# Other places in memory for the attention weights of a fused attention and feed-forward kernel, with the buffers rearranged that make room

## Chip, core and metric

The kernel runs on one core of a Trainium2 chip. The metric is the device time of one execution in microseconds (us); the kernel before took 703.69 us (median of three runs, 703.57 to 704.2).

## What is computed

A slot attention over 8 batches, 8 heads, 576 tokens, 64 dimensions and 32 slots is followed by a feed-forward layer of width 2048 with an ELU.

```
a = exp(phi - max over tokens);  a = a / (sum over tokens + 1e-9)
k_m, v_m = a^T k, a^T v                        # 32 slots per head
attn = softmax over slots of (q k_m^T / 8)
x = attn v_m                                   # all heads side by side, 4608 x 512
h = x w_in;  g = where(h > 0, h, exp(min(h, 0)) - 1)
out = g w_out                                  # 4608 x 512
```

## The kernel before

The values v_m of a batch are multiplied with `w_in` first (`vw`), so the hidden layer is the attention weights times `vw`. A batch has two halves of 288 tokens; a unit of work is one batch, one half and one of 16 tiles of 128 hidden channels: 256 units. From unit 8 on, every factor is split into a high and a low part in the fast float32 format, and a product is made of three passes: low weights with high stream, high with low, high with high (`PASSES`).

`hidden` (L1005) is the first matmul group of a unit: three passes for two groups of heads, six matmuls. The weights are `vw`; the stream is a part of the attention-weight tile `A`, whose shape is [128, group, high or low, 288] in 4-byte numbers. `elu_exp` (L1020, L1021, on ScalarE) makes the exponential into a buffer `gf` out of the accumulator `psh`; `elu_max` (L1029 or L1032, VectorE) finishes it in place; `elu_high` (L1044) and `elu_low` (L1050) split its first 256 tokens into `gp`. The last 32 tokens of a half are collected in `rest`, for the first batches by `rest_copy` on GpSimd (L1040), and are projected later with others (`rest_high`, `rest_project`). `project` (L1058) streams 512 columns of `wout` for two token tiles and three passes: six matmuls, with `gp` as weights. The units before number 8 use plain float32 for both (`hidden` L993, `project` L1077).

The order of all this is written out by hand: `ORDER` is a list of steps, each of which records its instructions, and every engine runs its own in that order. A pool gives a new tile the room of one whose readers have all been recorded, and the first writer of the new tile waits for them.

Small things around: `phi_max` and `phi_exp` leave a negated maximum and a sum per slot in `stats`; `slot_scale` makes the reciprocal `rinv`. From batch 2 on, the maxima go through DRAM and come back spread over all partitions in `nmx` (`send_max`, `spread_max`); `pick_max` copies the half that a partition needs to `nmb`, on GpSimd, and `e_shift` (L531, GpSimd) adds it to three thirds of a second copy of phi, loaded by `load_e` into tiles of the rotating tag `t2k`. `softmax_max` and `softmax_sum` keep maxima and sums of the attention weights in a tile `mx`.

In the built program the four A tiles begin on multiples of 256 bytes, before and after.

Of the kernel before, what the change touches and what calls it, by code (L numbers as in the profile page):

```python
# [8 lines left out]
F32 = mybir.dt.float32  # L9
F32R = mybir.dt.float32r  # L10
U32 = mybir.dt.uint32
AF = mybir.ActivationFunctionType
# [4 lines left out]
P = 128  # L17
B, H, S, D, M = 8, 8, 576, 64, 32
DM, DFF = 512, 2048
HALF = S // 2  # L20
# [4 lines left out]
UT = S // NU  # L25
SQ = 32
NSQ = 2 * UT // SQ
NB = 2
# [384 lines left out]
def fused_kernel(ctx: ExitStack, tc: tile.TileContext, phiT, phi, kv0, kvt, kv1, kv2, q0, q1, w_in, w_out, out):  # L413
# [8 lines left out]
    nc = tc.nc  # L422

    const = ctx.enter_context(tc.tile_pool(name="const", bufs=1))
    work = ctx.enter_context(tc.tile_pool(name="work", bufs=2))
# [5 lines left out]
    ident = const.tile([P, P], F32, name="ident")  # L431
# [4 lines left out]
    def t2k(shape, name):  # L436
        return work.tile(shape, F32, name=name, tag="t2k", bufs=7)

    tiny = work.tile([P, HALF], F32, name="gf", bufs=5)[:, 0:1]
    spare = [work.tile([P, 4 * CW], F32, name="spare", tag="vw", bufs=NVB) for _ in range(2)]
    SPARE = {"e0": 0, "e1": 512, "e2": 1024, "x0": 1536, "x1": 1664, "sc0": 2048, "sc1": 2368,
             "sc2": 2624, "sc3": 2944, "A320": 3200, "A321": 2048}
# [4 lines left out]
    def temp(b, name, i, n):  # L449
# [20 lines left out]
    st = [  # L470
        {"kv": {}, "q": {}, "vw": [None] * NVC, "A": [None, None], "e": {}, "sc": {}, "ps": {}}
        for _ in range(B)
    ]
# [24 lines left out]
        st[b]["ph"] = t  # L498

    def load_e(b, u):  # L500
        t = t2k([P, 3, P], "e")
        nc.sync.dma_start(t, phi[b - NB, :, 3 * u : 3 * u + 3])
        st[b]["e"][u] = t

    def send_max(b):

# [3 lines left out]
    def spread_max(b):  # L510

        s = st[b]
        d = s.pop("nmd")
        s["nmx"] = work.tile([P, P, 2], F32, name="nmx", bufs=1)
        nc.sync.dma_start(
            s["nmx"].rearrange("p x a -> p (x a)"),
            d.rearrange("x a -> (x a)").partition_broadcast(P),
        )

    def pick_max(b):  # L520

        s = st[b]
        s["nmb"] = work.tile([P, P], F32, name="nmb", bufs=1)
        for a in range(2):
            r = slice(a * TT, a * TT + TT)
            nc.gpsimd.tensor_copy(s["nmb"][r], s["nmx"][r, :, a])
# [139 lines left out]
    def phi_max(b, g=None):  # L666
        s = st[b]
        if "nm" not in s:
            s["nm"], s["sums"], s["rinv"] = (stats[:, b % 2, i] for i in range(3))
        g = slice(0, 2) if g is None else slice(g, g + 1)  # L670
        nc.vector.tensor_reduce(s["nm"][:, g], s["ph"][:, g], AX.X, ALU.max, negate=True)

# [7 lines left out]
    def slot_scale(b):  # L680
        s = st[b]
        sums = s["sums"]
        nc.vector.tensor_scalar(sums, sums, EPS, None, ALU.add)
        nc.vector.reciprocal(s["rinv"], sums)

    def e_transpose(b, u, where="b"):
# [132 lines left out]
    def turn(b, u, a):  # L819
# [5 lines left out]
        sc = s["sc"][u].rearrange("p n m -> p (n m)")  # L825
        nc.vector.transpose(sc[:, a * n : (a + 1) * n], s["ps"]["s", u][a])

    def softmax_max(b, u):
        sc = st[b]["sc"][u]
        n = sc.shape[1]  # L830
        t = work.tile([P, 2, 2 * UT // SQ], F32, name="mx")[:, :, :n]
        mx = t[:, 0]
        st[b]["sm", u] = t
        nc.vector.tensor_reduce(mx, sc, AX.X, ALU.max)  # L834
        st[b]["mx", u] = mx

# [11 lines left out]
    def softmax_sum(b, u):  # L848
        sc = st[b]["sc"][u]
        n = sc.shape[1]  # L850
        t = st[b].pop(("sm", u))
        sm = t[:, 1]
        nc.vector.tensor_reduce(sm, sc, AX.X, ALU.add)  # L853
        nc.vector.tensor_scalar(sm, sm, EPS, None, ALU.add)
        rs = sm
        nc.vector.reciprocal(rs, sm)
        st[b]["rs", u] = rs
# [32 lines left out]
            t0 = t1  # L890

    def new_A():
        return work.tile([P, 2, 2, HALF], F32R, name="A", bufs=4)

    def half_high(b, hf):
        s = st[b]
        s["A"][hf] = new_A()
        nc.scalar.copy(s["A"][hf][:, :, HI], s["A32"][hf])
# [5 lines left out]
    def probs_high(b, u):  # L904
        s = st[b]
        for hf, src, dst in probs_parts(b, u):
            if s["A"][hf] is None:
                s["A"][hf] = new_A()
            nc.scalar.copy(s["A"][hf][:, :, HI, dst], s["pr", u][:, :, src])
# [106 lines left out]

    def elu_exp(it):
        ps = gs[it]
        gf = work.tile([P, HALF], F32, name="gf", bufs=5)
        nc.scalar.activation(gf, ps, AF.Relu, scale=-1.0)  # L1020
        nc.scalar.activation(gf, gf, AF.Exp, scale=-1.0)  # L1021
        gs[it] = gf, ps
# [152 lines left out]
        eng = nc.scalar if p == B // 2 - 1 else nc.sync  # L1175
        eng.dma_start(rows, osbs.pop(("rest", p)))

    stats = work.tile([P, 2, 3, 2], F32, name="stats", bufs=1)
    work.tile([P, 2, 2 * UT // SQ], F32, name="mx")
    warm = ps_o.tile([P, P], F32, name="pso00")  # L1180

    def tables():
        nc.scalar.activation(tiny, ident[:, 0:1], AF.Exp)

    def warm_up(n):
        for _ in range(n):
# [5 lines left out]
    def pad(n):  # L1192
# [4 lines left out]
        f.__name__: f  # L1197
        for f in (
            tables, warm_up, pad, load_phi, load_e, load_kv, load_kv0, load_tail, load_q, load_half_q, load_raw, dec_mag,
            dec_low, dec_top, dec_add, dec_high, dec_rest, phi_max, phi_exp, slot_scale,  # L1200
            send_max, spread_max, pick_max, e_shift, e_exp, e_transpose, e_copy, slots, slots_copy, slots_transpose,
            kv_copy, all_scores, pair_scores, scores, turn, softmax_max, softmax_shift, softmax_exp, softmax_sum,
            softmax_divide, turn_back, probs_high, probs_low, vw, vw_copy, half_high, half_low, vw_high, vw_low, hidden,
            elu_exp, elu_max, rest_copy, elu_high, elu_low, project, project_part, collect_part, store_part, collect, store, rest_high, rest_low,
            rest_project, rest_collect, rest_store,
        )
# [53 lines left out]
```

## Time and profile before

| | |
|---|---|
| median of three runs | 703.69 us (703.57 to 704.2) |
| profiled execution | 703.95 us |
| its span, first to last instruction | 702.2 us |
| TensorE busy | 694.2 us, 99% |
| VectorE, ScalarE, GpSimd busy | 478.2, 461.4, 51.2 us |
| granted clock of TensorE | 1.000 of full speed |

Busy time of TensorE counts overlapping records once; a record lasts longer than the step to the next one. DMA moves 64.51 MB.

### The profile page before, as it was taken

To read this page: it belongs to the slowest core of one execution; us is meant where nothing else is said; L and a number is where in the kernel's file an instruction comes from. 1 tells how busy PE (TensorE), PEld (TensorE's weight loads), DVE (VectorE), ACT (ScalarE), POOL (GpSimd) and SP (SyncE) were. 2 spreads that over 40 slices of the span, in tenths; PEclk is the share of its full clock that TensorE was granted. 3 is DMA by queue.
4 is the path that set the end of the run, shared out by engine and by line. 5 is a ranking of instruction groups with operands and counts; after the bars stand their busy time and mean duration, and the time that the engine had idled before them with its cause. 6 is when DMAs were issued, how large, how long until landed. Compare 5 with 4: busy or idle time off the path is not lost.

```text
span 702.2 us, 14394 instructions
## 1 busy us (share of the span) xinstructions
PE 694.2 (99%) x5521; PEld 572.5 (82%) x5521; DVE 478.2 (68%) x1253; ACT 461.4 (66%) x1104; POOL 51.2 (7%) x100
## 2 busy tenths in 40 slices
PE   9999999999999999999999999999999999999997
PEld 8656787888788887888878888888878888888886
DVE  3999999896886488645954459644875457755443
ACT  3788898887665667756674557665675656756553
POOL 0011112113120002000100000200010000000000
PEclk9999999999999999999999999999999999999999
DMA  8992014434940534004211043103211010000001
GB/s 296 375 414 80 29 31 120 155 106 98 238 162 15 177 102 107 30 16 140 76 47 46 9 141 120 38 1 137 79 54 46 1 47 1 32 31 1 1 30 46
DMA packets 24261, 64.51 MB, mean 92 GB/s; under 512 B 3264, under 2 KB 6592, under 8 KB 24192
## 3 DMA queue, kind: packets, MB, share of 16 engines
q1 hardware_dynamic: 24048, 63.32, 27.6%
q8 instruction: 44, 0.72, 0.4%
q10 hardware_dynamic: 144, 0.26, 0.1%
q14 instruction: 25, 0.20, 0.1%
HBM read 54.13 MB, written 9.44 MB: 91 GB/s over the span
## 4 chain that ended last, share of the span: by engine, by line
PE 90%; DVE 7%; ACT 2%; issue 1%; POOL 0%; DVEq 0%; POOLq 0%
PE pso L1058 48%; PE psh L1005 27%; PE psb L1058 5%; PE psb L785 3%; PE psb L717 2%; PE pso L785 2%; PE pso L1187 1%; DVE top L626 1%; DVE gf L1029 1%; DVE win L650 1%; DVE top L625 0%; DVE mx L853 0%; ACT gf L1021 0%; DVE mx L834 0%; PE psb L770 0%
## 5 line engine op out<-in xcount | busy, mean ns | idle before, releaser
L1058 PE MATMUL pso<-wout,gp 128*128 128x512 f32 (+1 forms) x1515 | 389.2, 393 | 0.0
L1058 PEld LDWEIGHTS pso<-wout,gp 128*128 128x128 f32 x1515 | 270.1, 188 | 48.6 <-ACT gf L1021 1.7
L1005 PEld LDWEIGHTS psh<-A,vw 128*128 128x128 f32 x1488 | 220.3, 188 | 34.7 <-issue 6.1
L1005 PE MATMUL psh<-A,vw 128*128 128x288 f32 x1488 | 238.6, 296 | 0.6 <-DVE gf L1029 0.4
L1044 ACT CAST gp<-gf 128x256 fp32r<-128x256 f32 x248 | 100.2, 404 | 93.8 <-DVE gf L1032 77.0
L1032 DVE SCALAR_TENSOR_TENSOR gf<-gf,psh 128x256 f32<-128x256 f32 x192 | 80.3, 418 | 107.4 <-ACT gf L1021 106.4
L1020 ACT ACTIVATE gf<-psh 128x288 f32<-128x288 f32 x256 | 105.1, 410 | 70.6 <-PE psh L1005 67.4
L1050 DVE TENSOR_TENSOR gp<-gf,gp 128x256 fp32r<-128x256 f32 x248 | 107.8, 435 | 54.5 <-ACT gp L1044 53.6
L1021 ACT ACTIVATE gf<-gf 128x288 f32<-128x288 f32 x256 | 113.9, 445 | 8.1
L1058 PE MATMUL psb<-wout,gp 128*128 128x512 f32 x168 | 40.6, 389 | 0.0
L1033 DVE SCALAR_TENSOR_TENSOR rest<-gf,psh 128x32 f32<-128x32 f32 x192 | 39.2, 204 | 0.0
L531 POOL TENSOR_TENSOR e<-e,nmb 128x384 f32<-128x384 f32 x18 | 20.0, 1122 | 261.1 <-DVE gp L1145 128.5
L1040 POOL COPY rest<-gf 128x32 f32<-128x32 f32 x64 | 26.9, 420 | 161.2 <-DVE gf L1029 161.1
L1058 PEld LDWEIGHTS psb<-wout,gp 128*128 128x128 f32 x168 | 31.4, 188 | 6.5
L1029 DVE SCALAR_TENSOR_TENSOR gf<-gf,psh 128x288 f32<-128x288 f32 x64 | 28.7, 449 | 10.8 <-ACT gf L1021 10.0
L942 DVE TENSOR_TENSOR vw<-psb,vw 128x512 fp32r<-128x512 f32 (+1 forms) x46 | 26.6, 613 | 4.6 <-ACT vw L937 4.5
L937 ACT CAST vw<-psb 128x512 fp32r<-128x512 f32 (+1 forms) x46 | 22.3, 535 | 2.8 <-PE psb L785 2.7
L785 PE MATMUL psb<-win,kvm 64*32 64x512 f32 (+2 forms) x400 | 23.5, 522 | 0.2 <-DVE win L650 0.2
L1140 ACT CAST gp<-rest 128x256 fp32r<-128x256 f32 x32 | 13.0, 407 | 15.9 <-PE psb L1058 11.2
L626 DVE SCALAR_TENSOR_TENSOR top<-mag,top 128x512 uint32<-128x512 uint32 x32 | 22.2, 693 | 1.8 <-ACT mag L617 0.3
L621 ACT ACTIVATE mag<-raw 128x512 uint32<-128x512 uint32 x30 | 20.2, 676 | 4.7 <-DVE top L626 4.6
L617 ACT ACTIVATE mag<-raw 128x512 f32<-128x512 f32 x30 | 19.4, 662 | 0.4 <-DVE win L650 0.4
(124 smaller groups left out, 494.3 us busy)
## 6 DMA issues: line engine op xcount, KB each, us to landing
kvt<-kv SPq DMA_DIRECT2D x32, 512.0 KB, 6.5
raw<-w_in SPq DMA_DIRECT2D x15, 512.0 KB, 9.8
raw<-w_out SPq DMA_DIRECT2D x15, 512.0 KB, 9.9
out<-osb SPq DMA_DIRECT2D x15, 512.0 KB, 2.8
qt<-q SPq DMA_DIRECT2D x18, 384.0 KB, 4.7
ph<-phiT SPq DMA_DIRECT2D x7, 576.0 KB, 5.2
e<-phi SPq DMA_DIRECT2D x18, 192.0 KB, 4.6
qh<-q SPq DMA_DIRECT2D x4, 576.0 KB, 11.1
```

What stands on the lines that cost most here:

```text
L626: nc.vector.scalar_tensor_tensor(t, mags[k].bitcast(U32), 3, t, ALU.logical_shift_left, ALU.bitwise_or)
L785: nc.tensor.matmul(outs[a][32 * j : 32 * j + 32, :], lhs[r, 32 * j : 32 * j + 32], rhs[r, j], start=True, stop=True, tile_position=(64 * a ...
L1005: nc.tensor.matmul(ps, t[:, x, g, c0 : c0 + P], s["A"][hf][:, g, y, :], start=(n == 0), stop=(n == 5),)
L1020: nc.scalar.activation(gf, ps, AF.Relu, scale=-1.0)
L1021: nc.scalar.activation(gf, gf, AF.Exp, scale=-1.0)
L1029: nc.vector.scalar_tensor_tensor(gf, gf, -1.0, ps, ALU.add, ALU.max)
L1032: nc.vector.scalar_tensor_tensor(gf[:, :n], gf[:, :n], -1.0, ps[:, :n], ALU.add, ALU.max)
L1033: nc.vector.scalar_tensor_tensor(rest_of(b, j)[:, b % 2 * 2 + hf], gf[:, n:], -1.0, ps[:, n:], ALU.add, ALU.max)
L1040: nc.gpsimd.tensor_copy(rest_of(b, j)[:, b % 2 * 2 + hf], gf[:, NT * P :])
L1044: nc.scalar.copy(gp[:, HI], gs[it][:, : NT * P])
L1050: eng.tensor_tensor(gp[:, LO], gf[:, : NT * P], gp[:, HI], ALU.subtract)
L1058: nc.tensor.matmul(ps[:, cols], gp[:, y], wout[j][:, x, cols], start=(first and n == 0), stop=(last and n == 2),)
```

## The change

Each of the four parts of an `A` tile gets 32 numbers (128 bytes) of room ahead of it, so that a part begins at 128 modulo 256 bytes and, being 1152 bytes long, ends on a multiple of 256. Before, high parts begin at 0 and end at 128, low parts begin at 128 and end at 0.

The rest makes room. The exponential has four buffers, not five. The spread maxima of `pick_max` lie in a fourth third of the first phi tile instead of in `nmb`. Maxima and sums, and the softmax's `mx`, lie in one tile `small`, where a softmax sum takes the place of its maximum. The reciprocals of batches 2 and later lie behind the data in the tile of `nmx`, which is now one tile for all batches.

```diff
-    tiny = work.tile([P, HALF], F32, name="gf", bufs=5)[:, 0:1]
+    small = work.tile([P, 32], F32, name="small", bufs=1)
...
     def load_e(b, u):
-        t = t2k([P, 3, P], "e")
-        nc.sync.dma_start(t, phi[b - NB, :, 3 * u : 3 * u + 3])
-        st[b]["e"][u] = t
+        t = t2k([P, 3 + (u == 0), P], "e")
+        nc.sync.dma_start(t[:, :3], phi[b - NB, :, 3 * u : 3 * u + 3])
+        st[b]["e"][u] = t[:, :3]
+        if u == 0:
+            st[b]["nmb"] = t[:, 3]
+
+    tail = []
...
-        s["nmx"] = work.tile([P, P, 2], F32, name="nmx", bufs=1)
+        if not tail:
+            tail.append(work.tile([P, P + 2, 2], F32, name="nmx", bufs=1))
+        s["nmx"] = tail[0][:, :P]
...
-        s["nmb"] = work.tile([P, P], F32, name="nmb", bufs=1)
...
-            s["nm"], s["sums"], s["rinv"] = (stats[:, b % 2, i] for i in range(3))
+            n = 4 * (b % 2)
+            s["nm"], s["sums"] = small[:, n : n + 2], small[:, n + 2 : n + 4]
...
+        n = P + b % 2
+        s["rinv"] = sums if b < NB else tail[0][:, n]
         nc.vector.reciprocal(s["rinv"], sums)
...
+        turns_mx.append((b, u))
+        x = 8 + 12 * (len(turns_mx) % 2)
+        mx = small[:, x : x + n]
+        st[b]["sm", u] = mx
...
     def new_A():
-        return work.tile([P, 2, 2, HALF], F32R, name="A", bufs=4)
+        return work.tile([P, 2, 2, HALF + 32], F32R, name="A", bufs=4)[..., 32:]
...
     def elu_exp(it):
         ps = gs[it]
-        gf = work.tile([P, HALF], F32, name="gf", bufs=5)
+        gf = work.tile([P, HALF], F32, name="gf", bufs=4)
```

No engine's instructions change their order or number. What changes is the place of operands and some waits. ScalarE around the exponential of unit 6 before (the second L1020; `win` holds scores of batch 1 here, and names in brackets are the engines or queues waited for):

```order
L1020 ACTIVATE gf<-psh 128x288 [waits PE_49,Pool_49]
L1021 ACTIVATE gf<-gf 128x288 [waits Activation_49]
L909 CAST A<-win_79 128x2x128 [waits DVE_49]
L1020 ACTIVATE gf<-psh 128x288 [waits Pool_49]
L1021 ACTIVATE gf<-gf 128x288 [waits Activation_49]
L909 CAST A<-win_80 128x2x160
L846 ACTIVATE win_80<-win_80 128x256 [waits DVE_49]
L937 CAST vw<-psb 128x256 [waits PE_49] x2
```

The same place after, where the lines have moved down by 10 or 11:

```order
L1030 ACTIVATE gf<-psh 128x288 [waits PE_49,Pool_49]
L1031 ACTIVATE gf<-gf 128x288 [waits Activation_49]
L919 CAST A<-win_79 128x2x128 [waits DVE_49]
L1030 ACTIVATE gf<-psh 128x288 [waits PE_49]
L1031 ACTIVATE gf<-gf 128x288 [waits Activation_49]
L919 CAST A<-win_80 128x2x160
L857 ACTIVATE win_80<-win_80 128x256 [waits DVE_49]
L947 CAST vw<-psb 128x256 [waits PE_49] x2
```

The second exponential waited for a GpSimd copy out of its buffer; with four buffers it takes one that TensorE reads as weights (L1077), and waits for those matmuls.

## Rows read from the trace of the kernel before

**Rows 1.** The page's busy times (us, share, instructions) and granted clock in 40 slices.
```profile
PE 694.2 (99%) x5521; PEld 572.5 (82%) x5521; DVE 478.2 (68%) x1253; ACT 461.4 (66%) x1104; POOL 51.2 (7%) x100
...
PEclk9999999999999999999999999999999999999999
```

**Rows 2.** The chain that ended last, shares of the span by line.
```profile
PE pso L1058 48%; PE psh L1005 27%; PE psb L1058 5%; PE psb L785 3%; PE psb L717 2%; PE pso L785 2%; PE pso L1187 1%; DVE top L626 1%; DVE gf L1029 1%; DVE win L650 1%; DVE top L625 0%; DVE mx L853 0%; ACT gf L1021 0%; DVE mx L834 0%; PE psb L770 0%
```

**Rows 3.** Costliest groups: count | busy us, mean ns of one | idle before, releaser.
```profile
L1058 PE MATMUL pso<-wout,gp 128*128 128x512 f32 (+1 forms) x1515 | 389.2, 393 | 0.0
...
L1005 PE MATMUL psh<-A,vw 128*128 128x288 f32 x1488 | 238.6, 296 | 0.6 <-DVE gf L1029 0.4
```

**Rows 4.** Timeline of TensorE from 304.0: start us, us, instruction, count.
```profile
304.32 0.94 PE L1005 MATMUL psh<-A,vw 128*128 128x288 f32 x6
305.11 1.55 PE L1058 MATMUL pso<-wout,gp 128*128 128x512 f32 x6
306.49 0.94 PE L1005 MATMUL psh<-A,vw 128*128 128x288 f32 x6
```

**Rows 5.** Timeline of TensorE from 369.5, where projections follow each other.
```profile
369.54 5.61 PE L1058 MATMUL psb<-wout,gp 128*128 128x512 f32 x24
374.98 0.94 PE L1005 MATMUL psh<-A,vw 128*128 128x288 f32 x6
```

**Rows 6.** Groups at 304.35, at 304.50 (same row at 304.76), at 305.03.
```profile
L1005 PE MATMUL psh<-A,vw 128*128 128x288 f32 x1 | 0.3, 292 | 0.0
...
L1005 PE MATMUL psh<-A,vw 128*128 128x288 f32 x2 | 0.4, 294 | 0.0
...
L1005 PE MATMUL psh<-A,vw 128*128 128x288 f32 x2 | 0.4, 291 | 0.0
```

**Rows 7.** Groups at 305.28, 305.51 and 305.74, one projection each.
```profile
L1058 PE MATMUL pso<-wout,gp 128*128 128x512 f32 x1 | 0.4, 393 | 0.0
...
L1058 PE MATMUL pso<-wout,gp 128*128 128x512 f32 x1 | 0.4, 397 | 0.0
...
L1058 PE MATMUL pso<-wout,gp 128*128 128x512 f32 x1 | 0.4, 389 | 0.0
```

**Rows 8.** Groups of TensorE from 370 to 374.5.
```profile
L1058 PE MATMUL psb<-wout,gp 128*128 128x512 f32 x21 | 4.9, 389 | 0.0
```

**Rows 9.** Groups of TensorE from 318 to 328.
```profile
L1005 PE MATMUL psh<-A,vw 128*128 128x288 f32 x25 | 4.1, 293 | 0.0
```

**Rows 10.** Groups of TensorE from 614 to 640.
```profile
L1005 PE MATMUL psh<-A,vw 128*128 128x288 f32 x72 | 11.4, 294 | 0.0
```

**Rows 11.** Timeline of TensorE from 613.5, two unit starts three units apart.
```profile
632.53 0.95 PE L1005 MATMUL psh<-A,vw 128*128 128x288 f32 x6
...
639.05 0.95 PE L1005 MATMUL psh<-A,vw 128*128 128x288 f32 x6
```

**Rows 12.** Timeline of all engines from 48.5, around the exponential of unit 6.
```profile
48.84 1.88 PE L1077 MATMUL pso<-vw,gf 128*128 128x512 f32 x4
...
50.22 0.40 ACT L1020 ACTIVATE gf<-psh 128x288 f32<-128x288 f32 x1
...
52.33 0.74 DVE L942 TENSOR_TENSOR vw<-psb,vw 128x256 fp32r<-128x256 f32 x2
...
53.16 0.18 PEld L785 LDWEIGHTS psb<-win,kvm 64*32 64x32 f32 x16 [0.76 <-DVE vw L942]
```

**Rows 13.** Timeline of all engines from 304.3, low part and next exponential.
```profile
305.13 0.42 DVE L1050 TENSOR_TENSOR gp<-gf,gp 128x256 fp32r<-128x256 f32 x1
305.31 0.41 ACT L1020 ACTIVATE gf<-psh 128x288 f32<-128x288 f32 x1 [0.39 <-PE psh L1005]
```

**Rows 14.** Copies of L526 (min/median/max ns); GpSimd's timeline; DMA issues (KB, us to landing).
```profile
L526 POOL COPY nmb<-nmx x12: 284/294/559, 169.3 to 442.6; 64x128 f32<-64x128 f32 x12
...
343.57 1.32 POOL L531 TENSOR_TENSOR e<-e,nmb 128x384 f32<-128x384 f32 x1 [62.65 <-DVE gp L1145]
...
e<-phi SPq DMA_DIRECT2D x18, 192.0 KB, 4.6
```

More of the change, by code (lines that the diff above doesn't have):

```diff
@@ L826, in turn @@
         nc.vector.transpose(sc[:, a * n : (a + 1) * n], s["ps"]["s", u][a])
+    turns_mx = []
     def softmax_max(b, u):
@@ L830, in softmax_max @@
         n = sc.shape[1]
-        t = work.tile([P, 2, 2 * UT // SQ], F32, name="mx")[:, :, :n]
-        mx = t[:, 0]
-        st[b]["sm", u] = t
+        turns_mx.append((b, u))
+        x = 8 + 12 * (len(turns_mx) % 2)
+        mx = small[:, x : x + n]
+        st[b]["sm", u] = mx
         nc.vector.tensor_reduce(mx, sc, AX.X, ALU.max)
@@ L850, in softmax_sum @@
         n = sc.shape[1]
-        t = st[b].pop(("sm", u))
-        sm = t[:, 1]
+        sm = st[b].pop(("sm", u))
         nc.vector.tensor_reduce(sm, sc, AX.X, ALU.add)
@@ L1176, in rest_store @@
         eng.dma_start(rows, osbs.pop(("rest", p)))
-    stats = work.tile([P, 2, 3, 2], F32, name="stats", bufs=1)
-    work.tile([P, 2, 2 * UT // SQ], F32, name="mx")
     warm = ps_o.tile([P, P], F32, name="pso00")
     def tables():
-        nc.scalar.activation(tiny, ident[:, 0:1], AF.Exp)
+        nc.scalar.activation(small[:, 8:9], ident[:, 0:1], AF.Exp)
     def warm_up(n):
```

## The prediction

> **What bounds the kernel now.** I read the busy shares first: TensorE is busy 99% of the span at the full granted clock, which is the 2.4 GHz level [rows 1]. Its matmuls overlap in the records, so that share alone proves little; the chain that ended last says more: 48% of the span is the projection's matmul on it, 27% the hidden layer's, and other engines hold little [rows 2]. So the span is the sum of the steps from one matmul to the next, and what I must price is a step. The 1488 hidden matmuls of three-part products and the projections are the bulk [rows 3].
>
> A unit of work is six hidden matmuls (288 columns) and six projections (512 columns). In the timeline one starts at 304.32, its projections at 305.11, the next unit at 306.49: 0.79 + 1.38 = 2.17 us, without idle time [rows 4]. One stretch shows what a projection costs when no hidden matmul stands between: 24 of them from 369.54 to 374.98, that is 5.44 / 24 = 226.7 ns each [rows 5], and there each record lasts 389 ns [rows 8]. Record minus step is 162 ns, the tail that overlaps the next one; taken off a record, it leaves that matmul's own step. With this the records become a ruler in nanoseconds. Among units the projections' records are 393 on average instead of 389 [rows 3], and inside one unit 393, 397, 389 for the first three [rows 7]. Hidden records are 292 for the first, 294 on average for the first pair, 294 for the middle pair, 291 for the last pair [rows 6]; over a longer stretch 293 [rows 9]. A second, slower rhythm exists: from 632.53 to 639.05 three units take 2.173 us each with hidden records of 294 [rows 10, 11]. It comes and goes after an interruption and stays for many units, so the time of a step depends on a phase that one matmul hands to the next, and not on the shape alone.
>
> The price of the unevenness follows. Hidden: 293 − 291 = 2 ns x 1488 = 3.0 us. Projections: 393 − 389 = 4 ns x 1515 = 6.1 us. Together 9.1 us, the whole pool that a better phase could return if the cheapest seen records are the floor.
>
> **The change, part by part.** *The parts of A.* Before, a part is 1152 bytes long and the tile starts on a multiple of 256, so the high parts start at 0 and end at 128 modulo 256, the low parts start at 128 and end at 0. A unit streams high, high, low, low, high, high. After, every part is like the low one. No matmul is added or removed. If a stream that ends in the middle of a 256-byte block disturbs the next, the four high streams of a unit stop doing so. The rows do not decide it: the middle pair, which already lies as all will lie, reads 294, like the first pair and 3 ns worse than the last [rows 6]. That speaks against an own price of the place; but the slower rhythm shows that costs are handed on, so a stream may pay for its forerunner, and then the middle pair pays for the high pair ahead of it. From below the edit can be worth −9.1 us (everything even), from above +1.5 us (the last pair becomes like the middle one: 3 ns x 2 x 248) or, if each of the four converted streams rises from the cheapest record to the dearest hidden one (two of mean 294 with a first of 292 leave 296; 296 − 291 = 5 ns x 4 x 248), +5.0 us. I take the hidden matmuls' own unevenness as gone, −3.0 us, and leave the projections' where it is, because all operands of a projection keep their places modulo 256. That choice lies nearest to the rows that the edit touches directly.
>
> Here the Trainium skill speaks against the change: its page "TensorE: Matmul & The Clock Gate", section "Back-to-back issue gap", gives the warm step as columns / 2.4 + 2.5 ns, without any term for an address; that would be an estimated 122.5 and 215.8 ns, and this part of the sum would be 0. The trace does not agree on the size: the steps are about 130 and 231 ns [rows 4], and those of projections alone 226.7 [rows 5].
>
> *Four exponential buffers for five.* A buffer is filled at L1020 (305.31 in a unit) and last read by L1050 one unit later (305.13 + 0.42 + 2.17) [rows 4, 13]; so it is held for about 2.4 us, and with four it comes round again after 4 x 2.17 = 8.7 us. In the steady part this is free. In the start it is not: the order of ScalarE shows that the exponential of unit 6 now waits for TensorE. The buffer that it gets is read by the four records of L1077 that run from 48.84 to 50.72, while it started at 50.22 [rows 12]: 0.50 us late. Behind it on ScalarE stand a cast, the softmax exponential and the two copies of L937, then VectorE's L942, for which TensorE's weight loads wait at 53.16 [rows 12]. All are back to back, so I charge the whole 0.5 us, between 0 (later waits of the start swallow it) and 0.5.
>
> *Negated maxima in the first phi tile.* The two 0.3 us copies of pick_max [rows 14] now wait for the old contents of a rotating buffer, and so run later than they did. They need the buffer's release, not the load; the shift behind them on GpSimd waits for the load, which takes 4.6 us after its issue, and GpSimd had been idle 62.65 us there [rows 14]. Price 0; without that cover two copies in each of six batches, 0.6 us x 6 = 3.6 us on ScalarE's queue.
>
> *Small statistics in one tile, reciprocals in the tail of nmx.* The same instructions in the same order on the same engines; the sums overwrite maxima that VectorE has read just before. No load or store waits for more, apart from two phi loads that wait for a shift long past. Price 0, and tens of ns if one write has to wait. The row length of A (1280 for 1152 bytes) changes no shape of the copies that fill it: 0.
>
> **Sum.** The profiled execution took 703.95 us: span 702.2 and 1.75 around it; the median of the three runs is 703.69, 0.26 lower. 703.95 − 3.0 + 0.5 = 701.45, and against the median 701.2 us.
>
> **The rivals.** *All of it goes.* If the disturbance of projections is only the after-effect of the hidden streams, as the clean 389 of the stretch without them suggests [rows 8], both parts return: 703.69 − 9.1 + 0.5 = 695.1 us. For it: projections differ in nothing else in the two places. Against: a change by 128 bytes would have to remove every trace. Chance 0.20.
>
> *The place does not matter.* The unevenness then belongs to the position in the group or the weight loads, which stay: 703.69 + 0.5 = 704.2 us. For it: the middle pair's 294 equals the first pair's. Chance 0.22. This is what the skill's rule of the step would give.
>
> *A stream that starts in mid-block is the dear one.* Then four streams become dear that were not: +1.5 by the last pair, up to +5.0, so 703.69 + 0.5 + 1.5 = 705.7 us, at most 708.7. It decides from about 0.9 ns a converted stream on (0.9 us / 992, which with the 0.5 us of the start makes 1.4 us). For it: 291 against 294 within one unit. Against: the first pair starts at 0 and is no cheaper than the middle. Chance 0.23.
>
> My forecast, the hidden part alone, keeps 0.35.
>
> **How the numbers follow.** Three runs of this kernel lie within 0.1%; less than 0.2%, about 1.4 us, can't be told from no change. The forecast and "all of it" are faster: 0.55. "Does not matter" is the same: 0.22. Mid-block is slower: 0.23. The range goes from just below "all of it" to just above the first price of "mid-block", 694.8 to 706.0; outside lie a gain beyond the floor that I took and the dearer half of mid-block, about 0.2 together. The forecast's own range is 699.5 to 702.
>
> **What would show it.** Right: in steady units the hidden records fall from 293 to about 291 with pairs alike, and a unit from 2.17 towards 2.16 us; projections stay at 393. "All of it": projections at 389 too and units near 2.13. "Does not matter": the same 292, 294, 294, 291. Mid-block: the last pair at 294 or more. At the start, the exponential of unit 6 begins as the four L1077 records end, and TensorE reaches the matmuls of 53.16 half a microsecond later against the work before them. Wrong altogether would be a new idle time of TensorE in a steady unit, or a lasting change to the slower rhythm, which by its records (294 for 293 [rows 9, 10]) would cost 1 ns x 1488 = 1.5 us, whatever the place does to a single stream.

## The result and the profile after

The changed kernel takes 708.16 us (median of 6 runs, 707.47 to 709.45) against 703.73 us of the kernel before (6 runs, 703.53 to 704.46). The ratio is 1.0061, with a 95% interval of 1.005 to 1.0072: it is slower, outside the predicted range, on the side of the rival "a stream that starts in mid-block is the dear one". The profiled execution took 708.14 us, with a span of 706.3 us for 702.2 before.

The page of the changed kernel first: busy times, granted clock, and the two groups that answer to [rows 3] (count, then busy us and mean ns of one, then idle time ahead and what ended it).

```profile
PE 697.8 (99%) x5521; PEld 574.8 (81%) x5521; DVE 481.1 (68%) x1253; ACT 461.8 (65%) x1104; POOL 51.5 (7%) x100
...
PEclk9999999999999999999999999999999999999999
...
L1068 PE MATMUL pso<-wout,gp 128*128 128x512 f32 (+1 forms) x1515 | 389.5, 393 | 0.0
...
L1015 PE MATMUL psh<-A,vw 128*128 128x288 f32 x1488 | 241.1, 298 | 1.0 <-ACT e L542 0.4
```

TensorE has as many instructions as before and the same granted clock, but is busy 3.6 us longer. The projections read the same 393 ns. The hidden matmuls read 298 instead of 296 [rows 3]: with the ruler of the prediction 2 ns x 1488 = 3.0 us, the size of the forecast with the other sign.

The timeline of TensorE in the changed kernel (start us, us, instruction, count) answers to [rows 4]:

```profile
304.11 0.96 PE L1015 MATMUL psh<-A,vw 128*128 128x288 f32 x6
304.92 1.55 PE L1068 MATMUL pso<-wout,gp 128*128 128x512 f32 x6
306.30 0.95 PE L1015 MATMUL psh<-A,vw 128*128 128x288 f32 x6
307.10 1.54 PE L1068 MATMUL pso<-wout,gp 128*128 128x512 f32 x6
308.48 0.70 PE L1015 MATMUL psh<-A,vw 128*128 128x288 f32 x4
```

A unit takes 2.19 us (304.11 to 306.30), the next 2.18, where it took 2.17; no idle time stands in brackets behind a row. The hidden half has grown from 0.79 to 0.81 and 0.80, the projections stay near 1.38. Two longer stretches of three units, first of before, then of after:

```profile
319.26 0.95 PE L1005 MATMUL psh<-A,vw 128*128 128x288 f32 x6
...
325.76 0.95 PE L1005 MATMUL psh<-A,vw 128*128 128x288 f32 x6
```

```profile
321.31 0.96 PE L1015 MATMUL psh<-A,vw 128*128 128x288 f32 x6
...
327.87 0.95 PE L1015 MATMUL psh<-A,vw 128*128 128x288 f32 x6
```

6.50 against 6.56 us. I laid the starts of all 242 hidden groups of the two timelines beside each other and took the difference of each step to the next. The 236 steps that differ by at most 0.06 us add up to +3.3 us; up to 117 us they add almost nothing, and behind it about 0.3 us in every 50 us. One step is out of line: from 281.21 to 284.01, it adds 0.63 us. The other four steps above 0.06 add 0.16, and the first group starts 0.04 later. This makes 4.1, the difference of the spans.

The odd step first. All engines of the changed kernel around it:

```profile
276.66 3.45 POOL L536 TENSOR_TENSOR e<-e 128x384 f32<-128x384 f32 x3 [24.14 <-DMA e<-phi]
...
276.85 1.24 DVE L927 TENSOR_TENSOR A<-pr,A 128x384 fp32r<-128x384 f32 x1
...
284.01 1.04 PE L1015 MATMUL psh<-A,vw 128*128 128x288 f32 x6 [0.45 <-ACT e L542]
```

GpSimd's shift began 0.19 us ahead of VectorE's low part of A, and that took 1.24 us. What follows on VectorE and ScalarE moved back, until TensorE waited 0.45 us, by the profile for ScalarE's `e_exp` (L542). In another execution of the changed kernel, e7 below, the same instruction starts ahead of the shift:

```profile
276.46 0.55 DVE L927 TENSOR_TENSOR A<-pr,A 128x384 fp32r<-128x384 f32 x1
```

It takes 0.55 us, the shift starts at 277.01, and TensorE loses nothing there. The shift waits for its load in both, so this is a matter of when the load lands. The Trainium skill, page "SBUF — State Buffer", section "Who interferes with whom", says that a VectorE instruction with two inputs in SBUF contends with a GpSimd instruction that reads SBUF; 1.24 for 0.55 us agrees.

### The profile page after: what moved, and what is told of

Read it like the earlier page. It is cut to its first block, busy times and chain, and to the rows that moved or that the text cites. A ratio compares the mean times of both kernels' runs of the same rounds, so it can differ in the third digit from the quotient of the medians.

```text
span 706.3 us, 14395 instructions
## 1 busy us (share of the span) xinstructions
PE 697.8 (99%) x5521; PEld 574.8 (81%) x5521; DVE 481.1 (68%) x1253; ACT 461.8 (65%) x1104; POOL 51.5 (7%) x100
## 4 chain that ended last, share of the span: by engine, by line
PE 90%; DVE 6%; ACT 3%; issue 1%; POOL 0%; DVEq 0%; POOLq 0%; ACTq 0%
PE pso L1068 48%; PE psh L1015 27%; PE psb L1068 5%; PE psb L793 3%; PE psb L725 2%; PE pso L793 2%; PE pso L1195 1%; DVE top L631 1%; DVE gf L1039 1%; PE pso L1087 1%; DVE win L655 1%; ACT gf L1031 0%; DVE top L630 0%; ACT gf L1030 0%; ACT mag L626 0%
## 5 line engine op out<-in xcount | busy, mean ns | idle before, releaser
L1015 PE MATMUL psh<-A,vw 128*128 128x288 f32 x1488 | 241.1, 298 | 1.0 <-ACT e L542 0.4
L536 POOL TENSOR_TENSOR e<-e 128x384 f32<-128x384 f32 x18 | 19.9, 1120 | 62.0 <-DMA e<-phi 54.8
L531 POOL COPY e<-nmx 64x128 f32<-64x128 f32 x12 | 4.0, 330 | 245.8 <-PE psb L778 105.7
```

Source lines behind the costliest of these rows:

```text
L1015: nc.tensor.matmul(ps, t[:, x, g, c0 : c0 + P], s["A"][hf][:, g, y, :], start=(n == 0), stop=(n == 5),)
```

## The experiments

Four theories were tried for the 3.3 us that is spread over the units. **Mid-block (M):** a stream that starts at 128 modulo 256 bytes is dear, wherever the rest lies. **Seam:** a stream is dear that doesn't go on where, modulo 256, the one ahead of it ended. **Relative place (R):** what counts is where the stream lies against its weights. **Unit (U):** what counts is the whole sequence of places of twelve matmuls, and no simple distance prices it. The rival to all of these is that other edits, with their waits, cost the time. Rows of timelines below are start us, us, instruction, count; three units are the measure, because in the changed kernel single units alternate between 2.190 and 2.177 us.

### e1: the change without the room ahead of A's parts

```diff
-        return work.tile([P, 2, 2, HALF + 32], F32R, name="A", bufs=4)[..., 32:]
+        return work.tile([P, 2, 2, HALF], F32R, name="A", bufs=4)
```

> The whole change, but the parts of A stay where they were (rows of 288, no room ahead): four exponential buffers, the maxima in the phi tile and the joined small tiles remain. Mine (the place of the parts costs about 15 ns a unit): 703.7 to 704.3 us, units of 2.167 us again. Rival (the other edits cost it): about 708 us.

Measured: 704.51 us, ratio 1.0006 (0.9997 to 1.0015); three units (from 319.71 us) take 6.52 us, which is the kernel before in its slower rhythm [rows 11]; most of its other units take 2.167 us, as before. All edits but the place of A together cost at most 0.15%, so the place costs the rest.

### e2: the room behind the parts, all four at 0

```diff
-        ... name="A", bufs=4)[..., 32:]
+        ... name="A", bufs=4)[..., :HALF]
```

> As the change, with the 32 numbers of room behind each part, so that every part starts at 0 and ends at 128 modulo 256. Mid-block theory (a stream that starts in the middle of a 256-byte block is dear; before 2 of 6, changed kernel 6 of 6, about 0.9 us for each stream of the six): none starts there, 702.0 us. Seam theory (dear is a stream that starts at another place modulo 256 than where the one before it ended; before 4 of 6 seams, changed kernel 6 of 6, about 1.75 us a seam): 6 again, 707 us.

```profile
319.97 0.95 PE L1015 MATMUL psh<-A,vw 128*128 128x288 f32 x6
320.76 1.54 PE L1068 MATMUL pso<-wout,gp 128*128 128x512 f32 x6
322.13 0.95 PE L1015 MATMUL psh<-A,vw 128*128 128x288 f32 x6
...
326.45 0.95 PE L1015 MATMUL psh<-A,vw 128*128 128x288 f32 x6
```

Measured: 703.0 us, ratio 0.9987 (0.9978 to 0.9997). Three units take 6.48 us, a unit 0.79 for the hidden matmuls and 1.37 for the projections. The same buffers, the same waits, the same row length as in the change, and 5 us less: it is the place of the streams and nothing else. Here all six streams of a unit end at 128, in the middle of a block, and the unit is cheap.

### e3: before, with the high parts of both groups ahead of the low ones

```diff
-        return work.tile([P, 2, 2, HALF], F32R, name="A", bufs=4)
+        return work.tile([P, 2, 2, HALF], F32R, name="A", bufs=4).rearrange("p y g n -> p g y n")
```

Every stream now starts where the one ahead of it ended modulo 256: the starts alternate between 0 and 128.

> The kernel before with the two inner axes of A swapped in memory (high or low outside, group inside), so that group 0 lies at 0 and group 1 at 128 modulo 256 in both parts, and each stream starts where the one before it ended. No room added, nothing else changed. Seam theory: no seam left, 703.7 - 4 x 1.75 = 696.7 us. Mid-block theory: 3 of 6 start in mid-block instead of 2, 704.6 us. Place without effect: 703.7 us.

Measured: 704.78 us, ratio 1.0007 (0.9998 to 1.0016), three units (from 319.60 us) 6.52 us. The seam theory falls.

### e4: before, with high and low parts exchanged

```diff
-        nc.scalar.copy(s["A"][hf][:, :, HI], s["A32"][hf])
+        nc.scalar.copy(s["A"][hf][:, :, 1 - HI], s["A32"][hf])
...
-                    s["A"][hf][:, g, y, :],
+                    s["A"][hf][:, g, 1 - y, :],
```

(and so in the other places that write A). The unit streams from 128, 128, 0, 0, 128, 128.

> The kernel before with high and low parts of A swapped in memory: the four high streams of a unit lie at 128 modulo 256, the two low ones at 0. Mid-block theory: 4 of 6, 703.7 + 2 x 0.9 = 705.5 us. Seam theory: 4 seams of 6 as before, 703.7 us.

```profile
319.89 0.96 PE L1005 MATMUL psh<-A,vw 128*128 128x288 f32 x6
...
326.45 0.96 PE L1005 MATMUL psh<-A,vw 128*128 128x288 f32 x6
```

Measured: 706.06 us, ratio 1.0031 (1.002 to 1.0042), three units 6.56 us. That is the dearer of two rhythms here: about half of its unbroken units take 2.186 us, the others 2.173, each for many units on end, so its time lies below that of the change, whose three units take as long. At this point theory M had its numbers right twice (e3, e4). The next run asked whether it holds outside the kernel.

### e5: bursts of thirty equal matmuls behind the kernel before

The appended work isn't the reference's; it follows the last matmul, with all operands in place and TensorE alone at work.

```python
for o in (0, 8, 16, 24, 32, 40, 48, 56, 64):     # floats: 0 to 256 bytes
    burst("place", (o,), HALF)
burst("seamless", (0, 288), HALF)
...                                              # 256, 320, 512 columns at 0 and at 128 bytes
for o in (0, 32):
    burst("weights", (o,), HALF, w0=32)          # weights moved by 128 bytes
```

> The kernel before, with bursts of 30 matmuls appended that write nothing out: streams of the last A tile in the fast format, weights of 128 columns changed for each matmul. Places 0, 32, 64, ... 256 bytes at 288 columns; places 0 and 288 numbers in turn (each starts where the last ended); 256, 320 and 512 columns at 0 and at 128 bytes; 288 columns with the weights moved by 128 bytes too; then units of six matmuls of 288 (at 0, then at 128) and six of 512. Start in mid-block is dear: at 128 bytes 288, 256, 320 and 512 columns are all slower than at 0, the 288 by 2 to 3 ns a step, and places between lie between. End on a multiple of 256 is dear: 288 slower at 128, but 256, 320 and 512 slower at 0. Weights against stream: with both moved by 128 the price is gone. The kernel is longer by the bursts, about 100 us.

The timeline; a burst's step is the distance to the next start by 30.

```profile
697.55 4.12 PE L1207 MATMUL psb<-A,vw 128*128 128x288 f32 x30
701.50 4.17 PE L1207 MATMUL psh<-A,vw 128*128 128x288 f32 x30
705.51 4.13 PE L1207 MATMUL psb<-A,vw 128*128 128x288 f32 x30
...
713.42 4.16 PE L1207 MATMUL psb<-A,vw 128*128 128x288 f32 x30
717.43 4.16 PE L1207 MATMUL psh<-A,vw 128*128 128x288 f32 x30
...
737.35 3.76 PE L1207 MATMUL psb<-A,vw 128*128 128x256 f32 x30
740.94 3.77 PE L1207 MATMUL psh<-A,vw 128*128 128x256 f32 x30
744.54 4.56 PE L1207 MATMUL psb<-A,vw 128*128 128x320 f32 x30
748.94 4.56 PE L1207 MATMUL psh<-A,vw 128*128 128x320 f32 x30
753.34 6.99 PE L1207 MATMUL psb<-A,vw 128*128 128x512 f32 x30
760.16 7.15 PE L1207 MATMUL psh<-A,vw 128*128 128x512 f32 x30
767.16 4.16 PE L1207 MATMUL psb<-A,vw 128*128 128x288 f32 x30
771.16 4.11 PE L1207 MATMUL psh<-A,vw 128*128 128x288 f32 x30
775.11 0.95 PE L1207 MATMUL psb<-A,vw 128*128 128x288 f32 x6
```

With 288 columns, a burst at 0 takes 3.95 us, at 32 bytes 4.01, at 128 bytes 4.01: some 131.7 against 133.5 ns a matmul. With 512 columns it is 6.82 at 0 and 7.00 at 128. But 256 columns take 3.59 and 3.60, and 320 columns 4.40 at both places, so a start at 128 has no price of its own. Nor has an end on a multiple of 256: 512 columns end there from 0, their cheap place. And with the weights moved by 128 bytes too, the dear place is 0 (4.00) and the cheap one 128 (3.95): this made theory R.

The Trainium skill, page "TensorE: Matmul & The Clock Gate", section "Back-to-back issue gap", gives an isolated warm step of columns / 2.4 + 2.5 ns, an estimated 109 ns for 256 and 216 for 512 columns, and no term for a place. The trace does not agree: measured were 120, and 227 to 233. By these bursts alone, (columns + 32) / 2.4 comes out at 120.0, 133.3, 146.7 and 226.7 for the four lengths, which fits the bursts shown to 1 ns but for two kinds: 288 at a cheap place is 2 ns below, 512 at 128 bytes is 6 above.

### e6: all parts at 64 bytes

The slice of A in the change is `[..., 16 : 16 + HALF]`.

> As the change, with half of the room ahead and half behind, so that all parts start at 64 and end at 192 modulo 256 bytes. If any start off a multiple of 256 costs the same: 707 to 708 us as the change. If the price grows with the distance: between all at 0 and all at 128, 705 to 706. If only the half line counts: 703 us as all at 0.

Measured: 705.56 us, ratio 1.0016 (1.0008 to 1.0025), three units (from 319.79 us) 6.52 us: between the places 0 and 128. A price that grows with the distance from a multiple of 256 would give this too; e10, at 32 bytes, speaks against it.

### e7: the change once more

> The changed kernel once more, with a profile. If the 0.7 us that it lost between the units 88 and 96 (a GpSimd shift that met a VectorE subtraction) belongs to the change, it is lost again at that place; if it is where a load happened to land, it is elsewhere or gone. Steady units of 2.190 and 2.177 us again.

Measured: one time, 706.77 us, span 705.0. Three units from 319.89 take 6.54 us, again those of the change, and its small steps add up to +3.4 us against before; the step of 0.63 us at 281 us is not there, as shown above.

### e8: units measured by themselves

Behind the kernel before, six matmuls of 288 columns into one accumulator and six of 512 into another, six times over, in 23 settings of places; both stream from the last A tile with `vw` as weights. This is not part of the reference.

```python
def units(o1, w1, o2, w2):           # places in floats: hidden stream, weights; projection stream, weights
    for _ in range(6):
        group(ps_b, "psb", o1, HALF, w1)
        group(ps_h, "psh", o2, 512, w2)
units((0,), 0, (0,), 0)
units((0, 0, 32, 32, 0, 0), 0, (0,), 0)
units((0, 32), 0, (0,), 0)
units((32, 32, 0, 0, 32, 32), 0, (0,), 0)
units((32,), 0, (0,), 0)
units((32,), 32, (0,), 0)
units((0,), 32, (0,), 0)
...
units((32,), 32, (32,), 32)
for o in (8, 16, 24, 40, 48, 56):
    units((o,), 0, (0,), 0)
```

> The kernel before with stretches of synthetic units behind it (six hidden matmul groups into psb, six projections into psh each, as in the steady part, all operands resident), in 22 settings of the places of streams and weights modulo 256 bytes. What is appended is not part of the reference's computation; only the step from unit to unit counts. Theory R (a matmul is dear by the place of its stream relative to that of its weights): 2160 ns wherever streams and weights of a kind stand at the same place, also with both at 128 (the setting 32/32 floats); about 2190 and 2177 ns with the hidden streams at 128 and weights at 0, and the same with weights at 128 and streams at 0; the pattern of the kernel before (0, 0, 128, 128, 0, 0) at 2167 to 2173 ns. Theory M (a stream that starts in mid-block is dear, wherever the weights are): 2177 to 2190 with streams at 128 also where the weights are at 128, and 2160 with streams at 0 and weights at 128.

First rows of settings in the timeline; six units lie between the first row of one setting and that of the next, and between 790.45 and 829.81 two settings are left out.

```profile
698.96 0.95 PE L1205 MATMUL psb<-A,vw 128*128 128x288 f32 x6
...
711.93 0.94 PE L1205 MATMUL psb<-A,vw 128*128 128x288 f32 x6
...
724.93 0.95 PE L1205 MATMUL psb<-A,vw 128*128 128x288 f32 x6
...
737.97 0.96 PE L1205 MATMUL psb<-A,vw 128*128 128x288 f32 x6
...
751.09 0.96 PE L1205 MATMUL psb<-A,vw 128*128 128x288 f32 x6
...
764.19 0.95 PE L1205 MATMUL psb<-A,vw 128*128 128x288 f32 x6
...
777.29 0.96 PE L1205 MATMUL psb<-A,vw 128*128 128x288 f32 x6
...
790.45 0.95 PE L1205 MATMUL psb<-A,vw 128*128 128x288 f32 x6
...
829.81 0.95 PE L1205 MATMUL psb<-A,vw 128*128 128x288 f32 x6
...
842.87 0.96 PE L1205 MATMUL psb<-A,vw 128*128 128x288 f32 x6
...
855.83 0.95 PE L1205 MATMUL psb<-A,vw 128*128 128x288 f32 x6
...
868.87 0.96 PE L1205 MATMUL psb<-A,vw 128*128 128x288 f32 x6
```

Half of each distance is three units, to be laid beside the kernels:

| streams of the hidden matmuls | synthetic, 3 units us | in a kernel, 3 units us | ratio to before |
|---|---|---|---|
| all at 0 | 6.485 | 6.48 (e2) | 0.9987 |
| 0, 0, 128, 128, 0, 0 | 6.50 | 6.50 (before) | 1 |
| 0 and 128 in turn | 6.52 | 6.52 (e3) | 1.0007 |
| all at 64 | 6.52 | 6.52 (e6) | 1.0016 |
| 128, 128, 0, 0, 128, 128 | 6.56 | 6.56 (e4) | 1.0031 |
| all at 128, weights too | 6.55 | 6.55 (e9) | 1.0051 |
| all at 128 | 6.55 | 6.56 (after) | 1.0061 |
| all at 32 | 6.48 | 6.48 (e10) | 0.9975 |

The units alone, with no other engine at work and nothing to wait for, take what they take in these stretches of the kernels. The table leaves out the second rhythm of 2.173 us in before and e4, which the synthetic units don't show. Theory R falls: with streams and weights at 128 the units stay dear, and so they do with every operand at 128 (829.81 to 842.87, 13.06 us for six). Theory M falls as well: with the hidden streams at 0 and their weights at 128, where it has the cheap unit of 2.160 us, six units take 13.16 (777.29 to 790.45), 2.193 each and dearer than with the streams at 128. A burst doesn't price a unit either: streams at 32 bytes, dear in a burst, make the cheapest unit, and at 96 bytes, cheap in a burst (3.95), they make one as dear as at 128 (868.87 to 881.97, 6.55 for three). What is left is theory U, which is no formula: it foretells only what was measured as a whole unit. The rows of e9 and e10 come from the next two runs.

### e9: the change with the weights of the hidden matmuls at 128 as well

```diff
+    spare = [work.tile([P, 4 * CW], F32, name="spare", tag="vw", bufs=NVB) for _ in range(2)]
     small = work.tile([P, 32], F32, name="small", bufs=1)
-    spare = [work.tile([P, 4 * CW], F32, name="spare", tag="vw", bufs=NVB) for _ in range(2)]
```

> The changed kernel with the pools of the small statistics and of the spare value tiles taken in the other order, so that all vw tiles (the hidden matmuls' weights) also begin at 128 modulo 256, like the parts of A. Nothing else differs. Theory R (relative place): the steady units fall from 2190 and 2177 ns to 2160, and the time to about 703.0 us (702 to 704), as with all parts of A at 0. Theory M (mid-block start, wherever the weights are): no change, 707 to 708.2 us with units of 2190 and 2177 ns.

```profile
320.46 0.95 PE L1015 MATMUL psh<-A,vw 128*128 128x288 f32 x6
...
327.01 0.95 PE L1015 MATMUL psh<-A,vw 128*128 128x288 f32 x6
```

Measured: 707.3 us, ratio 1.0051 (1.0038 to 1.0065), three units 6.55 us: R's 703.0 is refuted in the kernel too. Its expectation was written before the result of e8.

### e10: all parts at 32 bytes

```diff
-        ... name="A", bufs=4)[..., 32:]
+        ... name="A", bufs=4)[..., 8 : 8 + HALF]
```

> The changed kernel with every part of an A tile at 32 modulo 256 bytes in place of 128. In the synthetic units a stream at 32 bytes made a unit of 2160 ns (hidden 801, projections 1359), as one at 0 did (787 and 1373), though its single hidden step is one of the dear ones. Theory U (what counts is the whole unit of six hidden and six projection matmuls, as measured by itself; no distance from a multiple of 256 prices it): units of 2160 ns with the halves 801 and 1359, and 703.0 us (702.4 to 703.7). Theory M (a stream that doesn't start on a multiple of 256 is dear): units of 2173 ns or more, 705 to 708 us. Theory R (the place relative to the weights): dear too, as the weights stand at 0, 705 to 708 us.

```profile
319.59 0.96 PE L1015 MATMUL psh<-A,vw 128*128 128x288 f32 x6
320.39 1.52 PE L1068 MATMUL pso<-wout,gp 128*128 128x512 f32 x6
321.75 0.96 PE L1015 MATMUL psh<-A,vw 128*128 128x288 f32 x6
...
326.07 0.96 PE L1015 MATMUL psh<-A,vw 128*128 128x288 f32 x6
```

Measured: 702.73 us (11 runs), ratio 0.9975 (0.9965 to 0.9985). M and R had 705 to 708; U's 703.0 came from e8 alone. It is the fastest kernel here, faster than before and than the change; its interval overlaps that of e2. The projections on its page:

```profile
L1068 PE MATMUL pso<-wout,gp 128*128 128x512 f32 (+1 forms) x1515 | 383.8, 389 | 0.0
```

The projections, none of whose operands moved, now read 389 on average for 393. A unit's halves are 0.80 and 1.36 us, for 0.79 and 1.38 before [rows 4]: the projections take less and the hidden matmuls more, so a place is paid for by neighbours too.

## Why the prediction was wrong

**The bound was right.** The span is the sum of TensorE's steps; the change moved the time through these steps, at the full clock and without idle time in the units.

**The failed step is "I take the hidden matmuls' own unevenness as gone, −3.0 us".** The edit added 3.3 us instead (e1 and e2 bracket it: 704.5 without it, 703.0 with the parts at 0, 708.2 with them at 128). Its premise was that a stream that ends in the middle of a block disturbs the next. In e2 all six end there and the unit is cheap, 2.16 us; in the change none does and the hidden half grows from 0.79 to 0.81 and 0.80 us. The one row on a stream at 128, the middle pair, was 3 ns worse than the last pair, and the prediction put this down to the high pair ahead of it. Such a record shows the place in company of four streams at 0, and not the place alone. The caution was in the text (costs are handed on from one matmul to the next) and was not applied to the choice.

**The pool of 9.1 us was not there either.** It added the cheapest hidden record (291) to the cheapest projection (389) as if both could be had at once. e2 and e10 show the trade: in both three units take 6.48 us, once as 0.79 and 1.37 a unit, once as 0.80 and 1.36. The lowest unit seen is 2.160 us, 7 ns below that of before: 7 ns x 248 units = 1.7 us is what the best of the places tried can bring, and the small steps of e10 add up to −1.8 us against before.

**The wait of the exponential was priced rightly.** The timeline of before, first, has one row more than [rows 12]; the rows of after follow.

```profile
53.75 0.70 PE L1077 MATMUL pso<-w,gf 128*128 128x512 f32 x1
```

```profile
48.46 1.88 PE L1087 MATMUL pso<-vw,gf 128*128 128x512 f32 x4
...
50.38 0.41 ACT L1030 ACTIVATE gf<-psh 128x288 f32<-128x288 f32 x1 [0.44 <-PE pso L1087]
...
53.79 2.41 PE L1087 MATMUL pso<-w,gf 128*128 128x512 f32 x5
```

The exponential waits for the four matmuls, as foretold, and from their start to the group behind it lie 5.33 us instead of 53.75 − 48.84 = 4.91: 0.42 us, forecast 0.5. All seven traces with four buffers have 5.32 or 5.33 there, all five with five buffers 4.91. In the spans it is hidden by chance, because the four matmuls themselves came 0.38 earlier; in e7, the same kernel, they came another 0.43 earlier. The run e1, which has this wait and not the new places, is 0.06% slower than before, 0.4 us, within what its interval can tell from nothing.

**The edits at price 0.** pick_max's copies and the small statistics are bounded by e1 together: between −0.2 and +1.1 us with the 0.42 of the wait in it. The longer rows are not in e1; they are in e2, which has all these edits and is faster than before. The copies ran where TensorE didn't wait for them, at 251.89 us for a shift at 276.66.

**The rivals.** "Mid-block" had the side and, with its 0.23, too small a chance; its upper price of +5.0 was nearer than the 1.5 that its time went by; with the 0.5 of the start, which its sum left out at the top, that is 709.2 us and not 708.7. Its mechanism isn't the cause (e5, e8, e10). "The place does not matter" and "all of it goes" fall with e2 and the change.

**What stays open.** Why a sequence of places costs what it costs is not settled. It is shown that the price belongs to the places of streams and weights within a unit, with everything else taken away (e8), and that it goes over to neighbours whose operands didn't move (e10). No formula for it came out of 23 settings, and why before and e4 have two rhythms isn't known either. A version with streams at 32 bytes and five exponential buffers, which might save the 0.42 us as well, was not tried.

## What to carry to other kernels

When matmuls follow each other without a gap, the start addresses of their operands can be worth about 1% of a step, as with the shapes here, and it can't be read off the records of one arrangement: a record that looks cheap may be paid for by its neighbour. Measure the repeating unit by itself, behind any kernel, for a list of offsets, and compare sums of whole units; eight settings measured in one run agree with stretches of the kernels to 0.01 us in three units, and one of them, all at 32, was measured ahead of its kernel. Price a gain against the lowest sum that was ever seen for the whole unit, and not against the lowest of each part.

## What was not expected of the hardware

- 512 columns: a matmul's step is 227 ns with the stream at 0 and 233 with it at 128 bytes, 256 and 320 columns are the same at both places, 288 columns differ by 2 ns (e5).
- Moving only the weights by 128 bytes exchanges which place of a 288-column stream is the cheap one in a burst (4.00 and 3.95 us for thirty), but moving streams and weights of a unit together does not bring back its cheap form (13.06 against 12.97 us for six, e8).
- The lowest unit, 2160 ns, is 6 x 320 + 6 x 544 = 5184 periods of 2.4 GHz, that is 32 more than the columns for each matmul; hidden streams at 0, 32 and 160 bytes reach it (e8), and the other arrangements of e8 lie 7 to 33 ns above it.
